# Two interleaved attention and FFT-filter layers on one core: which queue carries which rows, and where a few loads and transpositions stand in the order

## The chip, the core and the metric

The kernel runs on one core of one Trainium2 chip. The core has TensorE (PE in the profile) for matrix products and transpositions, VectorE (DVE), ScalarE (ACT) and GpSimd (POOL) for work on elements, and SyncE (SP), which only issues transfers. The metric is the device time of one launch in microseconds; the kernel before was timed in three runs.

## The reference

The input `x` has S = 2048 rows of D = 576 values, all in fp32. Four layers follow one another, attention and spectral filter in turn, each with a residual:

```
def _A_ref(x, wqkv, wo):                     # attention, 32 heads of 18, window W = 256
    q, k, v = (x @ wqkv) split into 3 x 32 heads
    scores = einsum("bhqd,bhkd->bhqk", q, k) * Dh ** -0.5
    scores = where(0 <= i - j < W, scores, -1e9)
    return einsum("bhqk,bhkd->bhqd", softmax(scores), v) merged @ wo

def _B_ref(x, w_r, w_i):                     # two-dimensional real FFT, a filter, and back
    X = rfft2(x, axes=(-2, -1)) * (w_r + 1j * w_i)
    return irfft2(X, s=(S, D), axes=(-2, -1))

x = x + _A_ref(layernorm(x), wqkv, wo)
x = x + _B_ref(layernorm(x), w_r, w_i)
x = x + _A_ref(layernorm(x), wqkv, wo)
x = x + _B_ref(layernorm(x), w_r, w_i)
```

## The kernel before

The order of the instructions on each engine is written by hand: the kernel records them one after another, and each engine works through its own in that order. Matrix products in fp32 accuracy are made from products of rounded values: an operand is split into a high part and a low part (`xh`, `xl`; `wqh`, `wql`), and two or three products are added.

**Transfers.** SyncE, ScalarE and GpSimd each issue transfers from their own place in the order. The transfers of SyncE and ScalarE together share eight completion semaphores, which are handed out in turn in the order of the program; a transfer is issued only when the one eight places earlier on that list, which has the same semaphore, has landed. GpSimd's transfers have eight of their own. What stands behind a waiting transfer on its engine waits too.

**Attention (`layer_a`).** The 2048 rows are 16 tiles of 128. In layer 1 `first_tiles` and the loop after it read each tile (`ld`), take its statistics (`bn`, `sq`, `bn2`), centre and scale it (`f0`, which gives `axn`), transpose it on TensorE (`f1`, tiles `tpaa` and `tpba`; ScalarE's and VectorE's casts give `xh` and `xl`) and make the value rows (`f2`, PSUM tile `vps`, stored to `v_d`). Then the projections of queries and keys run (`proj`, PSUM tile `pj`, copied through `sg` to memory `qk_d`). At their start ScalarE loads its table for the exponential by a one-column activation into the tile `ex`, and GpSimd builds the mask, clears parts of the key and query stacks by a long row of fills, and makes `wql`. In `opening` the first scores (`S`), their row maxima (`m`) and the remaining projections alternate; `m_rows` transposes four tiles of maxima (`tpm`), and ScalarE issues four transfers that put them into the query stack (`qs<-mt`). The exponentials are `E` (scores less the maximum, on TensorE) and `P` (ScalarE), the product with the values is `U`. At the end the attention's output blocks (`o_d` in memory) are loaded again by `out.load_o(u)`, GpSimd splits their last 64 columns, TensorE transposes them (`tpo`), and `out.unit` multiplies by `wo` (`ops`, 28 products); `out.load_x` loads the residual rows.

**Spectral filter (`layer_b`).** The transform along the 576 values is a product with cosine and sine tables; along the 2048 rows it is split as 16 x 128. *Forward columns*: for each tile n2 of 16, `f3` makes `pz` and `f4` the tile `ye` [128, 2 x 290]. It is stored to `yd[0][:, n2]` in memory. *Filter groups*: group g of 16 reads a tile of 128 rows, 8 from each n2 (`g0`), multiplies by `fc` (`g1m`, PSUM tile `p`), by the filter weights (VectorE, GpSimd: `uv`) and by `m` (`g2`, PSUM tile `pq`); the result (`ze` for odd, `eo` for even groups) goes to `yd[1][:, g]`. *Inverse*: tile n2 reads 128 rows, 8 of each group, into one of four places `yis` (`ly`), multiplies by `ga` (`i1`, PSUM tile `pi`), is transposed (`i2`, `tp`) and transformed back along the 576 values (`i3`, `po`).

At both changes of order between columns and groups the last results don't go through memory for all of their readers. From tile FD = 11 on, the eight rows of a tile that belong to groups 0 and 1 are sent straight into those groups' place in the on-chip memory ("rows", 8 x 580 values, 18.1 KB); rows of the tiles before come by one load. Likewise from group FG = 11 on the rows for the first `near` inverse tiles (two in layer 1, three in layer 2) are sent straight, and the older groups' rows come by two loads each, one of groups 0 to 7 and one of groups 8 to 10. All later groups and tiles load 128 rows from memory once every part of them is stored. While TensorE has nothing to do there in layer 2, it runs `warm` products whose result is not used; in layer 1 it prepares weights (`w1`, `w2`, PSUM tile `wo`) instead. In the profile the shared on-chip region in which the groups' places, `yis` and several other tiles lie is called `ofree` whatever tile it is.

## Time and profile before

| | us |
|---|---|
| three runs | 1385.17, 1386.48 (median), 1386.85 |
| the profiled execution | 1387.57 |
| its span in the profile | 1385.1 |
| TensorE busy in it | 1343.1 |
| VectorE busy | 893.3 |
| ScalarE busy | 785.4 |
| GpSimd busy | 640.0 |

TensorE's granted clock was 0.994 of full speed on average. In the rows below, a line of the order of time has its start, its duration, the engine, the line of the kernel, the operation, the tile written and the tiles read, and in brackets how long the engine had stood idle before it and what ended that. SPq, ACTq and POOL with DMA_DIRECT2D are the issue of transfers, and "xN" says that N like ones were merged. A row of waits has the waiting product, who was waited for, the total, the number of waits and the longest. A row of a stretch (A:B) has its length, the busy time of PE, PEld (weight loads), DVE, ACT and POOL with the number of instructions, the granted clock, the share of the DMA engines that was busy, and GB/s.

### The profile page before, as it was taken

How to read it: one execution, taken by the hardware profiler on the slowest of the kernel's cores; microseconds unless marked ns; L12 is line 12 of the kernel's file. 1: busy time of each engine (PE TensorE's matmuls, PEld its weight loads, DVE VectorE, ACT ScalarE, POOL GpSimd, SP SyncE). 2: the span in 40 equal slices, each digit the busy share in tenths (PEclk: the TensorE clock that was granted, in tenths of full speed). 3: DMA queues.
4: the chain of work that ended last, by engine and by line, in shares of the span. 5: the costliest groups of instructions: out<-in, count | busy, mean ns of one | idle time of the engine just before them, and what ended most of it. 6: DMA issues, size and time to landing. Idle time of an engine off the chain costs nothing.

```text
span 1385.1 us, 33553 instructions
## 1 busy us (share of the span) xinstructions
PE 1343.1 (97%) x11356; PEld 1001.1 (72%) x11356; DVE 893.3 (64%) x3046; ACT 785.4 (57%) x1978; POOL 640.0 (46%) x1140
## 2 busy tenths in 40 slices
PE   8999999999999999998999999999999999998988
PEld 8986666666665699975999866666666655897577
DVE  4417777877778266666673157787777883564745
ACT  5522777777778544443355316777777777563223
POOL 2257555555447443475221394554545457102711
PEclk9999999999999999999999999999999999999999
DMA  6756655655446457678763468555555465597864
GB/s 192 211 160 204 190 181 174 189 167 163 145 150 185 109 166 239 218 244 258 254 224 73 107 199 232 169 163 168 165 157 143 151 181 147 171 349 247 257 224 158
DMA packets 202159, 259.09 MB, mean 187 GB/s; under 512 B 104270, under 2 KB 109646, under 8 KB 201478
## 3 DMA queue, kind: packets, MB, share of 16 engines
q1 hardware_dynamic: 191494, 235.63, 55.8%
...
## 4 chain that ended last, share of the span: by engine, by line
PE 83%; DMA 5%; ACT 3%; DVE 3%; POOL 2%; issue 2%; SPq 1%; ACTq 0%; DVEq 0%; POOLq 0%
PE pj L1067 16%; PE S L1124 12%; PE U L1181 11%; PE vps L963 8%; PE ops L758 7%; PE E L1161 5%; PE po L251 4%; PE pq L488 2%; PE pf L251 2%; PE p L467 2%; PE tpo L1195 2%; PE pi L551 2%; ACT P L1162 2%; PE pz L289 2%; DMA yd<-ze 1%
## 5 line engine op out<-in xcount | busy, mean ns | idle before, releaser
L1126 DVE CUSTOM_DVE_ANT_0 jk<-S,mask 128x384 bf16<-128x384 f32 (+2 forms) x1024 | 490.4, 529 | 109.4 <-PE E L1161 56.1
L1162 ACT ACTIVATE P<-E 128x384 f32<-128x384 f32 (+2 forms) x1024 | 409.0, 476 | 121.9 <-PE E L1161 98.7
L1164 POOL TENSOR_SCALAR_AFFINE_SELECT P<-P 128x512 f32<-128x512 f32 x256 | 163.1, 637 | 277.9 <-ACT P L1162 254.3
L1124 PE MATMUL S<-ks,qs 63*128 63x384 f32 (+2 forms) x1024 | 269.1, 371 | 1.0 <-DVE m L1126 0.4
L1161 PE MATMUL E<-qs,ks 64*128 64x384 f32 (+2 forms) x1024 | 222.2, 372 | 3.3 <-ACT P L1162 2.6
L1124 PEld LDWEIGHTS S<-ks,qs 63*128 63x128 f32 x1024 | 140.7, 185 | 105.2 <-DVE m L1126 73.1
L1181 PE MATMUL U<-P,vq 128*19 128x128 f32 (+1 forms) x3840 | 187.8, 328 | 1.0 <-ACT us L1186 1.0
L1067 PE MATMUL pj<-xh,wqh 128*128 128x512 f32 x360 | 156.4, 434 | 3.3 <-DVE sg L1082 2.8
L1181 PEld LDWEIGHTS U<-P,vq 128*19 128x19 f32 x3840 | 95.7, 98 | 77.5 <-issue 21.7
L1167 POOL TENSOR_SCALAR_AFFINE_SELECT P<-P 128x512 f32<-128x512 f32 x224 | 142.8, 638 | 0.0
L1161 PEld LDWEIGHTS E<-qs,ks 64*128 64x128 f32 x1024 | 114.1, 185 | 17.0 <-ACT P L1162 8.2
L1067 PE MATMUL pj<-xh,wql 128*128 128x512 f32 x360 | 124.5, 419 | 0.5 <-POOL wql L648 0.5
L1067 PE MATMUL pj<-xl,wqh 128*128 128x512 f32 x288 | 122.1, 424 | 0.0
L758 PE MATMUL ops<-oroom 128*128 128x290 f32 (+1 forms) x812 | 116.3, 300 | 0.2
L758 PEld LDWEIGHTS ops<-oroom 128*128 128x128 f32 x812 | 111.4, 191 | 0.7 <-DVE ofree L781 0.7
L1067 PEld LDWEIGHTS pj<-xh,wqh 128*128 128x128 f32 x360 | 67.9, 189 | 34.8 <-issue 10.8
L1082 DVE TENSOR_TENSOR sg<-pj,sg 128x512 fp32r<-128x512 f32 x72 | 49.5, 687 | 58.3 <-ACT sg L1079 58.3
L1126 DVE DVE_READ_ACCUMULATOR2_ANT m<- 128x1 f32 x1024 | 85.2, 83 | 0.0
L1067 PEld LDWEIGHTS pj<-xh,wql 128*128 128x128 f32 x360 | 64.2, 189 | 20.9 <-issue 10.6
L1079 ACT CAST sg<-pj 128x512 fp32r<-128x512 f32 x72 | 42.2, 586 | 61.8 <-PE pj L1067 44.9
L243 ACT CAST et<-tp 128x512 fp32r<-128x512 f32 x53 | 31.2, 588 | 77.8 <-PE tp L239 76.7
L963 PE MATMUL vps<-wvh,xh 128*128 128x288 f32 x320 | 70.6, 302 | 0.2
...
## 6 DMA issues: line engine op xcount, KB each, us to landing
...
qs<-qk_d SPq DMA_DIRECT2D x384, 72.0 KB
...
```

Of the source, the lines that this page charges most:

```text
L251: T.matmul(ps[:, c, 0:NF], tail[r] if si == 4 else hl_(si), dcs[b // 2][r, b % 2], start=mi == si == 0, stop=si == 4)
L758: self.nc.tensor.matmul(self.ps[u][n][:, 0:self.n], x, self.w[p][:, (2 * wk + n) * self.n:(2 * wk + n + 1) * self.n], start=first and i == ...
L963: T.matmul(ps[:, n, 0:288], xT(xk, c), w[:, wk, n * 288:(n + 1) * 288], start=i == 0, stop=i == len(ks) - 1)
L1067: T.matmul(box["ps"].rearrange("r (n p) -> r n p", n=NT) if second else box["ps"], w[:, wk], x, start=s == 0, stop=s == len(ks) - 1)
L1082: V.tensor_sub(rest[:, 1], by, rest[:, 0].bitcast(F32))
L1124: T.matmul(ps[:, 0:N], q[b:b + 63, pair, i * 128:i * 128 + 128], k[b:b + 63, pair, lo:hi], start=True, stop=True)
L1126: V.tensor_tensor_reduce(out=jk[:, 0:N], in0=ps[:, 0:N], in1=mask[:, 384 - N:384], scale=1.0, scalar=-3e38, op0=ALU.add, op1=ALU.max, accu ...
L1161: T.matmul(ps[:, 0:nq], k[b:b + 64, pair, j * 128:j * 128 + 128], q[b:b + 64, pair, j * 128:j * 128 + nq], start=True, stop=True)
L1162: A.activation(p[:, hl_, 0:nq], ps[:, 0:nq], AF.Exp, scale=SC)
L1164: P.affine_select(out=p[:, :, 0:128], in_=p[:, :, 0:128], pattern=[[0, 4], [1, 128]], compare_op=ALU.is_ge, fill=0.0, base=0, channel_mult ...
L1167: P.affine_select(out=p[:, :, 256:384], in_=p[:, :, 256:384], pattern=[[0, 4], [-1, 128]], compare_op=ALU.is_gt, fill=0.0, base=0, channel ...
L1181: T.matmul(U[32 * h:32 * h + 19, (q0 % 4) * 128:(q0 % 4) * 128 + 128 * (q1 - q0)], vts[n][:, j, h], pt[n, j][:, h, (q0 - j) * 128:(q1 - j) ...
```

## The change

Six things change; the arithmetic stays.

1. *Groups to inverse tiles.* In layer 1 three tiles instead of two get their rows straight (`near` is 3 in both layers). GpSimd issues all rows for tile 2: of groups 11 to 13 in step 14, of groups 14 and 15 in step 15. In layer 2 that work was ScalarE's and, for group 15, SyncE's. The loads of groups 8 to 10 move from step 12 to step 13, behind the rows of group 12.
2. *Columns to groups in layer 2.* The rows of tiles 11 to 15 go to four groups, 0 to 3. So there are four rows a tile instead of two, a second load for the older tiles' rows, and no load for groups 2 and 3. Tile 13's rows and store are on GpSimd, tile 14's on ScalarE (recorded in the step of tile 15), tiles 11, 12 and 15's on SyncE; tile 15's store stands between its rows.
3. *`load_o(5)`* moves to the turn of the third block, ahead of the spectral layer, in both layers.
4. *`first_tiles`* in layer 1 holds `sq`, `bn2` and `f0` of tile 3, which came from the loop behind it.
5. *`ex`* is taken from the pool `bp` instead of `wp`.
6. *`m_rows`* in `opening` stands after three projection steps of the turn instead of after all seven.

In the order of SyncE in layer 2, from the columns to the groups, before: `ye` is the tile's result, `ofree<-ye` a row transfer, `yd0<-ye` the store, `ofree<-yd0` a load.

```order
L319 DMA ofree_17769<-ye11_19706 8x580 x2
L321 DMA yd0_18867<-ye11_19706 16x8x580
L327 DMA ofree_17769<-yd0_18867 88x2x580
L783 DMA x2_61<-ofree_17769 128x580
L319 DMA ofree_17769<-ye12_19777 8x580 x2
L319 DMA ofree_17769<-ye13_19791 8x580 x2
L319 DMA ofree_17769<-ye15_19813 8x580 x2
L321 DMA yd0_18867<-ye15_19813 16x8x580
L455 DMA ofree_17769<-yd0_18867 128x580 x2
L455 DMA ofree_17769<-yd0_18867 128x2x580 x5
```

And after:

```order
L321 DMA ofree_17775<-ye11_19712 8x580 x4
L326 DMA yd0_18874<-ye11_19712 16x8x580
L335 DMA ofree_17775<-yd0_18874 88x2x580 x2
L792 DMA x2_61<-ofree_17775 128x580
L321 DMA ofree_17775<-ye12_19786 8x580 x4
L326 DMA yd0_18874<-ye12_19786 16x8x580
L321 DMA ofree_17775<-ye15_19825 8x580 x2
L326 DMA yd0_18874<-ye15_19825 16x8x580
L321 DMA ofree_17775<-ye15_19825 8x580 x2
L464 DMA ofree_17775<-yd0_18874 128x580 x2
L464 DMA ofree_17775<-yd0_18874 128x2x580 x4
```

Tile 12 has four rows and its store on this queue, tile 13 none, tile 15 two more rows behind its store, and the two loads of 128 x 580 that were for groups 2 and 3 now serve groups 4 and 5.

On GpSimd at the same place, before (`ye<-half` is the subtraction that completes a tile):

```order
L653 TENSOR_TENSOR ofree_17769<-ofree_17769 128x64
L303 TENSOR_TENSOR ye12_19777<-half12_19765 128x290
L303 TENSOR_TENSOR ye13_19791<-half13_19792 128x290
L303 TENSOR_TENSOR ye14_19798<-half14_19799 128x290
L319 DMA ofree_17769<-ye14_19798 8x580 x2
L321 DMA yd0_18867<-ye14_19798 16x8x580
```

And after:

```order
L662 TENSOR_TENSOR ofree_17775<-ofree_17775 128x64
L303 TENSOR_TENSOR ye12_19786<-half12_19774 128x290
L303 TENSOR_TENSOR ye13_19803<-half13_19804 128x290
L321 DMA ofree_17775<-ye13_19803 8x580 x4
L326 DMA yd0_18874<-ye13_19803 16x8x580
L303 TENSOR_TENSOR ye14_19813<-half14_19814 128x290
L487 TENSOR_TENSOR uv0_19890<-ofree_17775 128x290
```

The five transfers of tile 13 now stand ahead of tile 14's subtraction, and tile 14's own have left this engine.

On SyncE in layer 1, from the groups to the inverse tiles, before: `ze` and `eo` are the groups' results (`eo2` is group 12's, `eo3` group 14's), `yd1` the memory between them, 24x580 the older groups' rows, 128x580 an inverse tile's load.

```order
L519 DMA ofree_7004<-yd1_8101 24x580 x2
L495 DMA ofree_7004<-eo2_8121 8x580 x2
L495 DMA ofree_7004<-ze13_10127 8x580 x2
L495 DMA ofree_7004<-eo3_8122 8x580
L495 DMA ofree_7004<-ze15_10153 8x580 x2
L525 DMA yd1_8101<-ze13_10127 16x8x580
L525 DMA yd1_8101<-ze15_10153 16x8x580
L164 DMA ofree_7004<-x0_59 128x1160
L545 DMA ofree_7004<-yd1_8101 128x580
L555 DMA x1_60<-ofree_7004 128x580
```

And after:

```order
L504 DMA ofree_7004<-eo2_8122 8x580 x2
L525 DMA ofree_7004<-yd1_8102 24x580 x3
L504 DMA ofree_7004<-ze13_10126 8x580 x2
L504 DMA ofree_7004<-eo3_8123 8x580
L504 DMA ofree_7004<-ze15_10158 8x580 x2
L534 DMA yd1_8102<-ze13_10126 16x8x580
L534 DMA yd1_8102<-ze15_10158 16x8x580
L164 DMA ofree_7004<-x0_59 128x1160
L564 DMA x1_60<-ofree_7004 128x580
L164 DMA ofree_7004<-x0_59 128x1160
L554 DMA ofree_7004<-yd1_8102 128x580
```

The rows of group 12 stand ahead of the older groups' loads, of which there are three instead of two, and the first load of 128 x 580 is tile 3's instead of tile 2's; it now stands behind tile 0's store to `x1`.

On SyncE in layer 2, at the end of the attention, before: `ofree<-o_d` of 128x448 is `load_o`.

```order
L724 DMA ofree_17769<-o7_d_10198 64x2048
L713 DMA ofree_17769<-o_d_10197 128x448
L724 DMA ofree_17769<-o7_d_10198 32x2048
L783 DMA x2_61<-ofree_17769 128x580 x3
L180 DMA ga_18890<-in_ga 128x256
L713 DMA ofree_17769<-o_d_10197 128x448 x3
L717 DMA ofree_17769<-x1_60 128x580
L783 DMA x2_61<-ofree_17769 128x580
```

And after:

```order
L722 DMA ofree_17775<-o_d_10204 128x448
L733 DMA ofree_17775<-o7_d_10205 32x2048
L722 DMA ofree_17775<-o_d_10204 128x448
L792 DMA x2_61<-ofree_17775 128x580 x3
L180 DMA ga_18897<-in_ga 128x256
L722 DMA ofree_17775<-o_d_10204 128x448 x2
L726 DMA ofree_17775<-x1_60 128x580
L792 DMA x2_61<-ofree_17775 128x580
```

One of the three loads behind `ga` stands ahead of the three stores to `x2` now.

The diff:

```diff
--- before.py
+++ after.py
@@ -138,7 +138,7 @@
     yd = [dram.tile([16, 16, 8, 2 * NF], F32, name=f"yd{j}") for j in range(2)]
     OPEN = *range(2, 17, 2), 17
     FD, FG, SH = 11, 11, 192
-    near, NY = (2, 3) if first else (3, 4)
+    near, NY = 3, 3 if first else 4
     with ExitStack() as stack:
         banks, inner = ExitStack(), ExitStack()
         ip = stack.enter_context(tc.tile_pool(name="bi", bufs=1))
@@ -148,7 +148,7 @@
         xfv, dstv = [a.rearrange("(p n) d -> p n d", n=NT) for a in (xf, dst)]
         xs, ys = {}, {}
 
-        pairs = [rl[:, 1160 * k:1160 * k + 1160] for k in range(4)]
+        pairs = [rl[:, 1160 * k:1160 * k + 1160] for k in (0, 3, 1, 2)]
         yis, tws = [[rl[:, at + 580 * k:at + 580 * k + 580].rearrange("p (a f) -> p a f", f=NF) for k in range(n)] for at, n in ((4640, 4), (6960, 2))]
 
         def y_tile(k):
@@ -305,26 +305,34 @@
                 both = ip.tile([128, 2, NF], F32, tag="both", name=f"half{n2}", bufs=2)
                 A.copy(both[:, 0], pz[:, 1, 0:NF])
                 if not first and n2 == NT - 1:
-                    for k in (n2 - 3, n2 - 2):
-                        hs[k]["store"](nc.scalar)
+                    hs[n2 - 1]["send"]()
                 V.tensor_add(ye[:, 0], pz[:, 0, 0:NF], both[:, 0])
                 V.tensor_sub(ye[:, 1], pz[:, 0, 0:NF], both[:, 0])
             yef = ye.rearrange("p j f -> p (j f)")
             pre(n2)
+            wide = 1 if first else 2
             if n2 == FD:
-                y_tile(0)
-            eng = P if n2 == NT - 2 else nc.sync
-            if n2 >= FD:
-                for g in range(2):
+                for k in range(wide):
+                    y_tile(k)
+            eng = nc.sync if n2 < NT - 3 or n2 == NT - 1 else P if first is (n2 == NT - 2) else nc.sync if first else nc.scalar
+
+            def rows(lo, hi):
+                for g in range(lo, hi):
                     eng.dma_start(ys[g][8 * n2:8 * n2 + 8].rearrange("p c f -> p (c f)"), yef[8 * g:8 * g + 8])
-            def store(q):
-                q.dma_start(yd[0][:, n2], yef)
-            if first or n2 not in (NT - 4, NT - 3):
-                store(eng)
+
+            def send():
+                if n2 >= FD:
+                    rows(0, 2 if n2 == NT - 1 else 2 * wide)
+                eng.dma_start(yd[0][:, n2], yef)
+                if n2 == NT - 1:
+                    rows(2, 2 * wide)
+            if eng is nc.scalar:
+                h["send"] = send
             else:
-                h["store"] = store
+                send()
             if n2 == FD:
-                nc.sync.dma_start(pairs[0].rearrange("p (a f) -> p a f", a=2)[0:8 * FD], yd[0][0:2, 0:FD].rearrange("a n i f -> (n i) a f"))
+                for k in range(wide):
+                    nc.sync.dma_start(pairs[k].rearrange("p (a f) -> p a f", a=2)[0:8 * FD], yd[0][2 * k:2 * k + 2, 0:FD].rearrange("a n i f -> (n i) a f"))
 
         def warm(n):
 
@@ -362,7 +370,7 @@
             f0(0, hs[0])
             for j in (1, 2, 3):
                 rims(j)
-            out.load(5)
+            out.load_x(5)
             norm(1)
             out.load(6)
             out.tail(5)
@@ -419,7 +427,8 @@
             zeros()
             norm(0)
             for u in (5, 6, 7):
-                out.load_o(u)
+                if u > 5:
+                    out.load_o(u)
                 out.tail(u)
             for u in (1, 2):
                 out.sums(u)
@@ -451,7 +460,7 @@
         def g0(g, h):
             if g % 2 == 0 and g not in ys:
                 y = y_tile(g // 2).rearrange("p a c f -> p a (c f)")
-                for a in ((0, 1), (1, 2)) if g == 2 else ((0, 2),):
+                for a in ((0, 1), (1, 2)) if g == (2 if first else 4) else ((0, 2),):
                     nc.sync.dma_start(y[:, a[0]:a[1]], yd[0][g + a[0]:g + a[1]].rearrange("a n i f -> (n i) a f"))
             h["y"] = ys[g]
 
@@ -500,23 +509,23 @@
                 V.tensor_sub(ye[:, 1], pq[:, 0, 0:NF], both[:, 1])
                 if first:
                     w1(3)
-                else:
-                    rows(nc.scalar, 2, 13)
-                    rows(nc.scalar, 2, 14)
-                for n2 in range(near):
+                for n2 in range(2):
                     rows(nc.sync, n2, 15)
+                for k in (14, 15):
+                    rows(P, 2, k)
                 held.pop()()
             else:
                 A.copy(both, pq[:, :, 0:NF])
-                if near > 2 and g in (FG + 1, FG + 2):
-                    rows(nc.scalar, 2, g - 1)
                 P.tensor_sub(ye[:, 1, 0:SH], both[:, 0, 0:SH], both[:, 1, 0:SH])
                 V.tensor_add(ye[:, 0], pq[:, 0, 0:NF], both[:, 1])
                 V.tensor_sub(ye[:, 1, SH:NF], pq[:, 0, SH:NF], both[:, 1, SH:NF])
-            if g in (FG - 1, FG + 1):
+            if g in (FG - 1, FG + 2):
                 lo, hi = (0, 8) if g < FG else (8, FG)
                 for n2 in range(near):
                     nc.sync.dma_start(yis[n2][8 * lo:8 * hi].rearrange("p c f -> p (c f)"), yd[1][n2, lo:hi].rearrange("g i f -> (g i) f"))
+            if g == 14:
+                for k in range(FG, 14):
+                    rows(P, 2, k)
             if FG <= g < 15:
                 for n2 in range(2):
                     rows(P if g == 14 and n2 else nc.sync, n2, g)
@@ -1006,6 +1015,9 @@
                 w_low(4)
                 bn(3, h[3])
                 f2(0, h[0], slice(1, 14))
+                sq(3, h[3])
+                bn2(3, h[3])
+                f0(3, h[3])
                 f2(1, h[1], slice(0, 8))
 
             if second:
@@ -1020,7 +1032,7 @@
                     if not second:
                         first_tiles()
                 for lag, fn in ((0, ld), (6 + late, f1), (4, sq), (4 + second, bn2), (4 + 2 * second, f0), (3, bn), (7 + late, f2)):
-                    if 0 <= s - lag < NT:
+                    if 0 <= s - lag < NT and (second or (s, lag) != (7, 4)):
                         fn(s - lag, hold[s - lag], *([slice(8, 14)] if s == 7 and lag == 6 and not second else []))
                 if s < 6 + late:
                     yield
@@ -1042,7 +1054,7 @@
                 q = wp.tile([128, 2, S], F32R, name=f"qs{j}", bufs=1)
                 k = wp.tile([128, 2, S], F32R, name=f"ks{j}", bufs=1)
                 qs.append(q); ks_.append(k)
-            A.activation(wp.tile([128, 1], F32, name="ex", bufs=1), eps, AF.Exp)
+            A.activation(bp.tile([128, 1], F32, tag="ex", name="ex", bufs=1), eps, AF.Exp)
 
             ended = []
 
@@ -1245,11 +1257,12 @@
                             score_max(t + LEAD, pair, hp)
                     remainders()
                     want = 7 * (t + LEAD + 1)
-                    yield from pj[n:want]
-                    n = want
                     y = t + LEAD - 1
+                    yield from pj[n:n + 3]
                     if y > 0 and y % 4 == 3:
                         m_rows(0, y // 4)
+                    yield from pj[n + 3:want]
+                    n = want
 
             def lasting(p):
                 x, half = p
@@ -1363,8 +1376,7 @@
                 if t - OB - 5 in (0, 1, 2):
                     u = t - OB - 5
                     out.turn(u, pp.tile([128, 512], F32, tag="pj", name=f"tpa{u}", bufs=1), V)
-                    if u < 2:
-                        out.load_o(u + 3)
+                    out.load_o(u + 3)
                 if t == NX:
 
                     A.activation(wp.tile([128, 1], F32, name="se", bufs=1), eps, AF.Sqrt)
```

## The prediction

> **What bounds the kernel now.** I read the share of busy time first, then TensorE's waits over the whole run, then the order of time around each place that the diff touches. The profiled execution took 1387.57 us (span 1385.1 us and 2.47 us around it), 1.09 us above the median 1386.48 us of the three runs, which spread from 1385.17 to 1386.85; so a difference under about 0.2% (2.8 us) can't be told from none.
>
> ```profile
> PE 1343.1 (97%) x11356; PEld 1001.1 (72%) x11356; DVE 893.3 (64%) x3046; ACT 785.4 (57%) x1978; POOL 640.0 (46%) x1140
> ...
> PE pi L551 <- DMA ofree<-yd: 4.3, 2, 3.0
> ...
> PE pj L1067 <- POOL wql L648: 0.5, 1, 0.5
> ```
>
> TensorE is busy 1343.1 of 1385.1 us. No part of the change removes arithmetic from it, so everything to be won lies in the 42 us in which it stands, and in stretches where its clock has dropped after such a stop. A wait row gives the total, the count and the longest; the two shown are the largest and a small one that decides a term below. The change touches many such stops, each at another place, so the sum has many small terms, and each place's rows stand with it.
>
> **First tiles of layer 1.** The centring of tile 3 now stands ahead of the casts of tile 2.
>
> ```profile
> 14.67 0.21 DVE L918 BATCH_NORM_AGGREGATE mv<-st 128x2 f32<-128x12 f32 x1
> 17.71 0.69 DVE L662 TENSOR_TENSOR xl<-tpaa,xh 128x512 fp32r<-128x512 f32 x1 [2.84 <-ACT xh L661]
> ...
> 19.62 0.66 PE L659 MATMUL tpaa<-ident,axn 128*128 128x128 f32 x4 [0.87 <-ACT axn L929]
> ```
>
> The tile's statistics are ready at 14.88 (14.67 + 0.21), but VectorE stands 2.84 us for the other tile's cast before it takes the next step of tile 3. With the order turned, the normalised tile is there some 2 us sooner and the stop of 0.87 goes. The cast, some 0.3 us late then, lies beside TensorE's value matmuls. Term: -0.9 (between -0.5 and -0.9).
>
> **The exp-table load.** Its small output tile `ex` no longer takes the memory of tiles that the stores to `v_d` read, so ScalarE needn't wait for them.
>
> ```profile
> 84.28 1.28 ACT L1045 ACT_TABLE_LOAD   x1 [4.20 <-DMA v_d<-vt]
> ...
> 87.09 0.50 PE L1067 MATMUL pj<-xh,wqh 128*128 128x512 f32 x1 [1.42 <-DVE sg L1082]
> ...
> 84.56 0.42 POOL L1035 MEMSET mask<- 128x384 bf16 x1 [13.61 <-DMA v_d<-vt]
> ...
> 108.35 1.54 POOL L648 TENSOR_TENSOR wql<-wqr,wqh 128x640 fp32r<-128x640 f32 x1
> ...
> 790.39 0.51 PE L1067 MATMUL pj<-xh,wqh 128*128 128x512 f32 x1 [0.60 <-DVE sg L1082]
> ```
>
> In layer 1 the stop of 1.42 goes, but it is not won: GpSimd's chain from the mask at 84.56 to `wql` at 108.35 also starts at those stores' landing, isn't touched, and TensorE already waits 0.5 for its end (the last wait row above). TensorE comes there 1.42 earlier and waits 1.9. In layer 2 the stop is 0.60, and no wait on `wql` is listed there (its count is 1), with no row for how near it is; I take half. Term: -0.3 (0 to -0.6).
>
> **The row of maxima.** The transposition `tpm` and what follows from it are recorded four projection matmuls sooner.
>
> ```profile
> 129.12 3.01 ACTq L1144 DMA_DIRECT2D qs<-mt  x4
> ...
> 129.55 1.07 PE L1067 MATMUL pj<-xh,wql 128*128 128x512 f32 x4
> 133.20 0.44 PE L1161 MATMUL E<-qs,ks 64*128 64x384 f32 x1 [1.59 <-ACT P L1162]
> ...
> 837.03 0.44 PE L1161 MATMUL E<-qs,ks 64*128 64x384 f32 x1 [1.01 <-ACT P L1162]
> ```
>
> ScalarE spends 3.01 us issuing the four transfers of the maxima; the cast and the exponentials stand behind them, and TensorE waits 1.59 and, in layer 2, 1.01. The same issue begins 4 matmuls earlier, about 0.23 us each by the start-to-start in the group of four that takes 1.07, so 0.9. It is a shift of ScalarE's queue with nothing before it that would be late. Term: -0.9 twice, -1.8 (-1.2 to -1.9).
>
> **The load of the sixth output block (`load_o(5)`) in layer 2.** It moves from the bunch of three at 1191.70 to the turn of the block before it.
>
> ```profile
> 1191.70 1.40 SPq L713 DMA_DIRECT2D ofree<-o_d  x3
> ...
> 1189.66 4.05 PE L758 MATMUL ops<-oroom 128*128 128x290 f32 x28
> 1195.05 0.52 PE L733 MATMUL tpo<-ident,ofree 128*128 128x128 f32 x3 [1.34 <-DMA ofree<-o_d]
> 1196.13 0.33 PE L734 MATMUL tpo<-ident,ofree 128*128 128x128 f32 x1 [0.56 <-POOL ofree L653]
> ...
> 1197.70 4.97 PE L758 MATMUL ops<-oroom 128*128 128x290 f32 x28
> ...
> 1195.00:1200.00 5.00, 4.39 (x21) 4.19 (x22) 3.55 (x9) 4.07 (x14) 2.00 (x6) 0.66 0.23 78
> 1200.00:1255.00 55.00, 55.00 (x419) 55.00 (x418) 36.50 (x97) 33.32 (x94) 4.50 (x16) 1.00 0.98 341
> ```
>
> Two stops, 1.34 for the load and 0.56 for GpSimd's split of it, are gone when it is there early. Behind them the granted clock was 0.66 (a stretch's row ends with the granted clock, the share of the DMA engines and GB/s), and the 28 matmuls took 4.97 where the 28 before took 4.05: another 0.92. By these rows the edit is worth up to 2.8; I take 2.7, as the clock may drop a little without them too. The lower end is 1.9, the stops alone. Late next are the loads of blocks 6 and 7, issued about as now and wanted one and two rounds of 28 matmuls later. Term: -2.7 (-1.9 to -2.8). In layer 1 the same move meets no stop in the rows, so 0.
>
> The Trainium skill ("TensorE: Matmul & The Clock Gate", Part 1: The HAM clock gate) says that the clock falls to half only after a window of about 3.4 us without work. Here stops of 1.34 and 0.56 us with work between were enough for 0.66, so the trace doesn't agree; by the page the drop would have another cause and stay, and this term would be -1.9 and the sum 0.8 smaller.
>
> **Layer 1, filter groups to inverse tiles.** Tile 2 now gets its rows like tiles 0 and 1 and needs no load of 128 rows; GpSimd issues them. The older groups' loads stand behind the rows of group 12.
>
> ```profile
> 643.74 1.35 SPq L495 DMA_DIRECT2D ofree<-eo  x2
> ...
> 647.32 1.30 SPq L495 DMA_DIRECT2D ofree<-ze  x2
> ...
> 653.26 0.34 SPq L545 DMA_DIRECT2D ofree<-yd  x1
> ...
> 649.47 2.20 PE L551 MATMUL pi<-ofree,ga 128*128 128x290 f32 x8 [1.75 <-DMA ofree<-ze]
> ...
> 657.22 2.22 PE L551 MATMUL pi<-ofree,ga 128*128 128x290 f32 x4 [3.02 <-DMA ofree<-yd]
> ...
> 662.48 1.14 PE L551 MATMUL pi<-ofree,ga 128*128 128x290 f32 x4
> ```
>
> Row group 12 (1.35) now goes out while SyncE still waits to issue the older loads, of which there is one more (some 0.3): the last rows, now at 647.32, come about 1.0 sooner, and with them tiles 0 and 1 (stop 1.75). Tile 2 no longer waits for the load issued at 653.26, so its stop of 3.02 goes, and its four matmuls, slow after that stop (2.22 against 1.14 for tile 3's), gain 1.1. Together 5.1. The first load that still is one is tile 3's. It takes the place of tile 2's, a little earlier, and lands about 4 us after issue as that one did (653.26 to 657.22), near 656. It now stands behind tile 0's store in the queue, which waits for that tile's sum, near 651 by the row of 649.47 less 1.0, and so isn't later for it; tile 3 is then due at 662.48 - 5.1 = 657.4. That is tight, so I take -4.5. If GpSimd's seven transfers land as late as the removed load did, only the first 1.0 is left. Term: -4.5 (-1.0 to -5.2). From tile 3 on TensorE is the bound, so what is won there stays.
>
> **Layer 2, the same place.** It had three such tiles already; new are GpSimd as issuer, one row less at the end of SyncE's queue and the loads' place.
>
> ```profile
> 1313.42 1.59 SPq L495 DMA_DIRECT2D ofree<-eo  x2
> ...
> 1317.25 1.98 SPq L495 DMA_DIRECT2D ofree<-ze  x3
> ...
> 1323.95 0.80 SPq L545 DMA_DIRECT2D ofree<-yd  x2
> ...
> 1329.79 1.25 PE L551 MATMUL pi<-ofree,ga 128*128 128x290 f32 x4 [1.25 <-DMA ofree<-yd]
> ```
>
> The pair at 1313.42 (1.59) goes into an idle time ahead, and the third of the rows at 1317.25 (1.98 / 3 = 0.66) leaves the queue: 2.25 less ahead of the last store, on whose landing the load at 1323.95 waits, and that load ended TensorE's wait at 1329.79. The tiles ahead of it start sooner by the same rows, about 1.4. Term: -2.1 (-0.5 to -2.3).
>
> **Layer 2, columns to filter groups.** The rows of tiles 11 to 15 go to four groups, not two; so the load for groups 2 and 3, after the last store, is not needed. The price is ten more row transfers, on three queues.
>
> ```profile
> 1261.14 6.67 SPq L319 DMA_DIRECT2D ofree<-ye  x6
> 1269.26 0.58 SPq L321 DMA_DIRECT2D yd<-ye  x1
> 1272.44 9.29 SPq L455 DMA_DIRECT2D ofree<-yd  x6
> ...
> 1263.06 1.52 ACTq L321 DMA_DIRECT2D yd<-ye  x2
> ...
> 1263.88 1.12 POOL L319 DMA_DIRECT2D ofree<-ye  x2 [0.29 <-DMA ofree<-yd]
> ...
> 1269.66 0.71 PE L467 MATMUL p<-ofree,fc 128*64 128x290 f32 x4 [2.16 <-DMA ofree<-ye]
> ...
> 1271.64 1.19 PE L467 MATMUL p<-ofree,fc 128*64 128x290 f32 x8
> 1275.36 2.20 PE L467 MATMUL p<-ofree,fc 128*64 128x290 f32 x8 [2.53 <-DMA ofree<-yd]
> ```
>
> Today groups 0 and 1 start at 1269.66 after a stop of 2.16, group 2 at 1275.36 after 2.53. After the change tile 13's four rows and store stand on GpSimd ahead of tile 14's subtraction: 5 x 0.56 = 2.8, so tile 14's transfers, now on ScalarE, begin near 1263.88 + 2.8 = 1266.7, last row at 1269.0, store at 1269.7 (0.76 each). SyncE issues tile 12's and 15's rows, and the eight completion semaphores go round over SyncE's and ScalarE's transfers in the order of the program: a transfer waits until the one eight places before has landed. So tile 12's second row waits for tile 14's first, and tile 15's for the last of them. With landings of 2 to 3 us (the last of the six rows ends its issue at 1267.81 and the data is used at 1269.66; the store issued at 1269.26 lets the load go at 1272.44) tile 15's first two rows go at about 1271.7 and 1272.4, and group 0 starts near 1274.2: 4.5 later. The stop of 2.53 then is gone, but TensorE has stood 6.7 us (since 1269.66 - 2.16 = 1267.5) and starts slow, as group 2 does now (2.20 for eight matmuls, 1.19 for the eight before). The matmuls of groups 0 and 1, 3.2 us now (1269.66 to 1272.83), take about 4.8, slow for most of it, so group 2 comes at 1279.0, 3.6 later than now, and no longer slow: 2.20 - 1.19 = 1.0 back. Term: +2.5. Bounds: -4.7, both stops gone; +5.0, all of the delay and the slow start.
>
> **Sum.** -0.9 - 0.3 - 1.8 - 2.7 - 4.5 - 2.1 + 2.5 = -9.8, so 1387.57 - 9.8 = 1377.8 for a profiled execution, and 1376.7 beside the median.
>
> **Rivals.** (a) The last hand-over works as it was drawn: the rows land in time, both stops go. For it, each row transfer is small; against it, the chain over the shared semaphores. 2.5 + 4.7 = 7.2 less: 1369.5. (b) GpSimd's rows for the third inverse tile land late, and both places at the inverse yield 1.5 together in place of 6.6: 1381.8. For it, the last of them are issued behind six others; against it, they start about 9 us before tile 2 is due. (c) From 1200 to 1255 the DMA engines were 0.98 busy: when TensorE arrives 2.7 earlier they are the bound and the gain of `load_o(5)` is given back: 1379.4. Against it, TensorE had no gap in those 55 us. (d) Slower: the waits on the shared semaphores in the hand-over from columns to groups stand in a row instead of beside each other, six issues of SyncE (three rows and the store of tile 12, two rows of tile 15) at a landing of 3.2 (1269.26 to 1272.44), 19 us, of which the rows of now already fill 2: +17 in place of +2.5, 1391.2. It decides from a loss of 12.3 on, where the other terms are used up, and needs group 0 to start after about 1284.
>
> **How the numbers follow.** The forecast 50%, (a) 15%, (b) 16%, (c) 10%, (d) 9%. The range reaches from (a) to somewhat above (b), where (b) and (c) fall together with the upper bound of the hand-over: 1369.5 to 1385.0; only (d) is left out. Faster 86%: all but (d), less the upper edge of (b); same 5%, slower 9%.
>
> **What would show it.** Right: no wait for `axn` of 0.87 near 19.6, none of 1.4 near 87 but about 1.9 for `wql` near 108; the exp wait of 1.59 down to 0.7; `tpo` near 1195 without a stop and the clock there near 1.0; `pi` of tile 2 in layer 1 without a wait and of tile 3 about 5 us sooner beside the work before it; group 0 of layer 2 later and group 2 without a stop. Wrong: tile 2's `pi` waits for a row from GpSimd, or the stop ahead of group 0 is far longer than 6.7 us, or short.

## The result, and the profile after

| | runs | median, us | ratio to before, 95% |
|---|---|---|---|
| before, on the same chip | 14 | 1385.38 | |
| changed | 14 | 1384.74 | 0.9996 (0.9984 to 1.0008) |
| changed, beside the first experiments | 12 | 1382.50 (before 1382.37) | 0.9995 (0.9979 to 1.0011) |

Nothing that can be told from no change, where 9.8 us were forecast. The profiled execution of the changed kernel took 1384.23 us (span 1382.3). The page's busy times and the waits of TensorE on the changed kernel:

```profile
PE 1341.2 (97%) x11356; PEld 998.3 (72%) x11356; DVE 892.7 (65%) x3046; ACT 786.9 (57%) x1978; POOL 646.4 (47%) x1152
...
PE p L476 <- DMA ofree<-ye: 8.7, 1, 8.7
PE pj L1079 <- POOL wql L657: 2.4, 2, 1.9
...
PE tpo L742 <- ACT ofree L799: 1.1, 1, 1.1
PE E L1173 <- DMA qs<-mt: 1.1, 2, 0.9
...
PE pi L560 <- DMA ofree<-yd: 1.1, 1, 1.1
```

The stops that were to go did go: no 3.0 for the inverse load of layer 1, none of 1.4 at the first projection copies, none of 1.3 for the sixth output block. Others stand in their place, with other names: 8.7 ahead of the filter groups of layer 2 (2.2 and 2.5 before), 1.9 for `wql` (0.5 before), 1.1 for ScalarE one output block later, 0.9 for a transfer of the maxima, 1.1 for the next inverse load.

One profile doesn't tell how much each of these counts. So all later runs were compared stretch by stretch. A stretch's length is the start of one product less the start of an earlier one, the same two products in every profile; stretches are named by these starts in the first profile of before. The fifth column is the mean of the profiles that have the part less the mean of those that have it not, with the number of profiles of each in brackets.

| stretch, us | before, three profiles | changed, two | that part undone | mean with less mean without (profiles) | forecast |
|---|---|---|---|---|---|
| 14 to 112, first tiles and exp table | 98.8, 98.9, 98.8 | 99.3, 99.6 | 98.8 | -0.4 (11, 5) | -0.9 |
| 125 to 141, maxima, layer 1 | 16.0, 15.8, 14.7 | 14.1, 14.1 | 14.3 | -0.9 (13, 5) | -0.9 |
| 640 to 664, groups to inverse, layer 1 | 23.5, 22.4, 23.7 | 21.3, 20.5 | 22.8 | -1.9 (12, 4) | -4.5 |
| 815 to 888, maxima, layer 2 | 73.0, 75.2, 73.6 | 74.7, 75.3 | 73.7 | +1.2 (13, 5) | -0.9 |
| 1190 to 1204, sixth output block | 14.5, 12.3, 12.2 | 12.0, 12.0 | 12.2 | -0.8 (14, 4) | -2.7 |
| 1255 to 1280, columns to groups, layer 2 | 25.2, 23.8, 23.2 | 29.2, 28.4 | 24.3 | +4.6 (9, 4) | +2.5 |
| 1304 to 1331, groups to inverse, layer 2 | 27.0, 28.5, 26.1 | 24.2, 24.0 | 26.3 | -3.2 (14, 4) | -2.1 |

The means are over all profiles, of the experiments too, that have that part or have it not; profiles in which an experiment alters the same place in another way are left out. They add up to -1.4, within the interval of the measured time (-0.6, from -2.2 to +1.1). Outside these stretches the profiles differ too: from 141 to 640 by up to 3.6 us between one execution and another of kernels that are alike there, from 888 to 1140 by up to 3.3. Kernels below for which no ratio is given ran once, for their profile; a single time says little where 14 runs of one kernel spread over 6 us.

### The profile page after: what moved, and what is told of

Its sections match the earlier page's. It is cut to its first block, busy times and chain, and to the rows that moved or that the text cites. A ratio compares the mean times of both kernels' runs of the same rounds, so it can differ in the third digit from the quotient of the medians.

```text
span 1382.3 us, 33597 instructions
## 1 busy us (share of the span) xinstructions
PE 1341.2 (97%) x11356; PEld 998.3 (72%) x11356; DVE 892.7 (65%) x3046; ACT 786.9 (57%) x1978; POOL 646.4 (47%) x1152
## 4 chain that ended last, share of the span: by engine, by line
PE 81%; POOL 4%; DMA 4%; ACT 4%; DVE 3%; issue 3%; SPq 1%; ACTq 0%; DVEq 0%; POOLq 0%
PE pj L1079 15%; PE S L1136 12%; PE U L1193 11%; PE vps L972 8%; PE ops L767 7%; PE E L1173 5%; PE po L251 4%; PE p L476 2%; PE pf L251 2%; PE tpo L1207 2%; PE pi L560 2%; PE pq L497 2%; ACT P L1174 2%; POOL qs L1227 2%; POOL ks L1226 2%
## 5 line engine op out<-in xcount | busy, mean ns | idle before, releaser
L1079 PEld LDWEIGHTS pj<-xh,wql 128*128 128x128 f32 x360 | 64.8, 190 | 23.5 <-issue 10.7
```

The costliest lines, as they stand in the source:

```text
L1079: T.matmul(box["ps"].rearrange("r (n p) -> r n p", n=NT) if second else box["ps"], w[:, wk], x, start=s == 0, stop=s == len(ks) - 1)
```

## Experiments

**Once more the changed kernel, and twice more the one before.**

> The changed kernel once more, beside the experiments, to see which small differences between the two profiles come back. If the profile of the changed kernel can be relied on to a few tenths at a place, the stop ahead of group 0 in layer 2 is again 8.7 us (8.2 to 9.2), the one for wql in layer 1 1.9, the one for the maxima's transfer near 883 0.9, and the inverse of layer 1 gives back 1.1 at tile 3. If these are of one execution only, they differ by half or more. Time against before: 0.998 to 1.001.

> The kernel before once more, for a second profile of it. Two profiles of the changed kernel differed by 1.7 us in span, and in single waits for transfers of the attention by up to 1.6. If the first profile of before was an ordinary one, this one's span is within 1 us of 1385.1 and its stops are the same at each place; if it was a slow one, the span is 1380 to 1383 and the difference lies in the waits for transfers, not at the places of the change.

> The kernel before a third time. Its first two profiles differ by 1 to 3 us in single stretches (648 to 664: 1.1; 842 to 888: 1.6; 1190 to 1204: 2.2; 1255 to 1280: 1.5; 1304 to 1331: 1.5). If the second was the ordinary one, the third has no drop of the clock near 1195 and takes about 12.0 from 1190 to 1204; if the first was, it has the drop again and takes 14.

Spans 1384.0, 1385.4 and 1382.4 us. At the first repeat the stops of 8.7, 1.9 and 0.9 came back as 8.1, 1.9 and 1.3, the 1.1 at inverse tile 3 only as 0.4. The second expectation was half wrong: the span was as long as the first, but the length lay elsewhere, two of the changed places among them. The third's span was 3 us shorter, and it too had no drop of the clock near 1195. What the table shows for before is therefore no fixed number at any place where a transfer's landing decides.

**The columns' rows for two groups again.**

```diff
-                    hs[n2 - 1]["send"]()
+                    for k in (n2 - 3, n2 - 2):
+                        hs[k]["store"](nc.scalar)
...
-                for k in range(wide):
-                    y_tile(k)
+                y_tile(0)
...
-            if eng is nc.scalar:
-                h["send"] = send
+            if first or n2 not in (NT - 4, NT - 3):
+                store(eng)
```

> The changed kernel with the rows of layer 2's columns for two groups again, as before the change; all else stays. Theory 1: this part costs 4.3 us (group 3's products stood at -4.2 ahead of it and +0.1 behind it in the profiles), so without it the kernel takes 1380 to 1381, ratio 0.996 to 0.998, with a stop of about 2.2 ahead of group 0 and 2.5 ahead of group 2. Rival: what this place gains or loses is made up later, at the inverse tiles whose loads wait for the last store; then the time stays within 1 us of the changed kernel's.

1379.71 us, ratio 0.9975 (0.9957 to 0.9993): without this part the rest of the change is a gain of some 3 us. That is 2.8 under the changed kernel's 1382.50, where theory 1 had 4.3, and the intervals of the two ratios overlap; the time alone wouldn't settle it. The stretch does: from 1255 to 1280 it is 24.3 instead of 29.2 and 28.4, with stops of 2.06 and 3.17 in place of the one of 8.66. Theory 1 holds at this place.

**Where the 4.6 come from.** The changed kernel at that place, SyncE, ScalarE, GpSimd and TensorE in order of time, then a stretch's row, then the chain of work that ended last there (start, duration, what):

```profile
1259.27 9.63 SPq L321 DMA_DIRECT2D ofree<-ye  x4
1269.62 1.30 SPq L321 DMA_DIRECT2D ofree<-ye  x2
...
1262.88 2.78 ACTq L321 DMA_DIRECT2D ofree<-ye  x4
...
1259.49 2.09 POOL L321 DMA_DIRECT2D ofree<-ye  x4 [0.41 <-DVE ye L302]
...
1272.43 1.24 PE L476 MATMUL p<-ofree,fc 128*64 128x290 f32 x4 [8.66 <-DMA ofree<-ye]
...
1268.00:1276.00 8.00, 3.57 (x16) 2.15 (x18) 0.00 (x0) 0.00 (x0) 0.00 (x0) 0.57 0.48 122
...
1262.88 4.01 DMA ofree<-ye
...
1266.92 0.63 SPq L321
...
1269.62 2.47 DMA ofree<-ye
```

SyncE spends 9.63 us on the four rows of tile 12: it stands until the first row of tile 14, issued by ScalarE at 1262.88, has landed 4.01 us later, on the semaphore they share. Tile 15's rows follow at 1269.62, land after 2.47, and TensorE, which stood 8.66 us, goes on at a clock of 0.57. Four other orders of the same transfers tell whether the semaphores or the transfers are at fault.

GpSimd's transfers of tile 13 behind the subtraction of tile 14:

```diff
                 P.tensor_sub(ye[:, 1], both[:, 0], both[:, 1])
+                if n2 == NT - 2:
+                    hs[n2 - 1]["send"]()
...
-            if eng is nc.scalar:
+            if not first and n2 in (NT - 3, NT - 2):
                 h["send"] = send
```

> The changed kernel with one thing put in another order: tile 13's five transfers on GpSimd stand behind the subtraction of tile 14, not ahead of it. Theory 1 (the delay of 2.8 us of tile 14's rows passes through the shared semaphores to tile 12's and 15's rows): tile 14's rows on ScalarE begin 2.9 us sooner, SyncE's rows follow, group 0 starts 2.5 to 3.5 sooner, the stop falls from 8.7 to about 5.5, time 1381 to 1382.5. Rival (the many small transfers themselves land late, whatever their order): the stop stays over 7.5 and the time within 1 us of the changed kernel's.

1383.22 us, ratio 1.0011 (0.9995 to 1.0027). ScalarE's order of time, the chain, and TensorE's:

```profile
1257.65 2.83 ACTq L323 DMA_DIRECT2D ofree<-ye  x4
...
1260.52 7.01 DMA yd<-ye
...
1267.59 2.04 DMA ofree<-ye
...
1269.87 1.24 PE L478 MATMUL p<-ofree,fc 128*64 128x290 f32 x4 [8.35 <-DMA ofree<-ye]
```

ScalarE's rows do start sooner (warm products end at about 1261.5 here, 1263.8 in the changed kernel), and nothing is won: now it is ScalarE's store of tile 14 that takes 7.01 us to land, and tile 15's rows go out on SyncE when it has. As a forecast this missed, and the rival's two numbers came true (a stop over 7.5, a time within 1 us). The rows show the mechanism of theory 1 with another transfer to wait for; the next two runs tell the two apart.

Tiles 13 and 14 both on GpSimd, nothing on ScalarE:

```diff
-            eng = nc.sync if n2 < NT - 3 or n2 == NT - 1 else P if first is (n2 == NT - 2) else nc.sync if first else nc.scalar
+            eng = P if n2 == NT - 2 or not first and n2 == NT - 3 else nc.sync
...
-                if not first and n2 == NT - 1:
-                    hs[n2 - 1]["send"]()
```

> The changed kernel with tiles 13 and 14 both on GpSimd, all ten transfers behind tile 14's subtraction, and none of them on ScalarE. With tile 13's transfers moved alone the stop ahead of group 0 had stayed (8.35): SyncE's rows of tile 15 then waited 7.0 us for tile 14's store on ScalarE. Theory 1 (SyncE's rows are held by landings of another engine's transfers through the shared semaphores): with no transfer of ScalarE among them SyncE issues the rows of tile 15 by about 1263 (1269.6 in the changed kernel), and group 0 then waits only for GpSimd's rows: stop 4 to 6.5. Rival (the rows land late since the transfers as a whole take that time): the stop stays over 7.5.

```profile
1258.88 2.69 SPq L321 DMA_DIRECT2D ofree<-ye  x4
...
1262.51 2.77 SPq L321 DMA_DIRECT2D ofree<-ye  x2
...
1268.85 0.84 PE L476 MATMUL p<-ofree,fc 128*64 128x290 f32 x4 [3.89 <-DMA ofree<-ye]
```

The four rows of tile 12 take 2.69 us instead of 9.63, and the stop is 3.89. The same number of rows is moved. So the larger part of the stop came through the shared semaphores, and the rival, which had a stop over 7.5, falls. Slow landing is what is left: seven of GpSimd's eight rows took 4.5 to 5.7 us to land here.

The rows of all four tiles ahead of all their stores, tiles 13's and 14's stores on ScalarE:

```diff
+                h["rows"] = lambda: rows(0, 4)
+                if n2 != NT - 3:
+                    rows(0, 4)
+                if n2 == NT - 1:
+                    for k, q in ((12, nc.sync), (13, nc.scalar), (14, nc.scalar), (15, nc.sync)):
+                        hs[k]["store"](q)
```

> As the run with both tiles on GpSimd, and the four tiles' rows stand ahead of all their stores: tile 12's and 15's stores on SyncE behind its rows, 13's and 14's on ScalarE behind. Theory 1: nothing that SyncE's rows wait for is in flight but their own forerunners, and the stores of 290 KB are no longer ahead of them; group 0 starts 4 to 6 us sooner than in the changed kernel and groups 2 and 3 follow without a stop; time 4 to 5 us under the changed kernel's, ratio to before 0.996 to 0.998. Rival (small transfers are slow in themselves, 4 to 6 us each): stop over 6, gain under 2.

```profile
1260.67 6.21 DMA yd<-ye
...
1266.96 2.32 DMA ofree<-ye
...
1272.07 1.24 PE L484 MATMUL p<-ofree,fc 128*64 128x290 f32 x4 [6.95 <-issue]
```

1384.50 us, ratio 1.0006 (0.9987 to 1.0025): a miss again, once more with the rival's numbers, and the clearest row of all for the semaphores. "Ahead" held only on each queue: ScalarE, which had nothing else to do, sent a store at 1260.67, and SyncE's first row of tile 12, whose data had long been ready, stood until that store had landed 6.21 us later.

GpSimd issues the eight rows of tiles 13 and 14, SyncE all the rest, stores last (the lines are against the run before):

```diff
-                    for k, q in ((12, nc.sync), (13, nc.scalar), (14, nc.scalar), (15, nc.sync)):
+                    for k, q in ((12, nc.sync), (13, nc.sync), (14, nc.sync), (15, nc.sync)):
...
+                    for lo in (0, 2):
+                        for k in (n2 - 1, n2):
+                            hs[k]["rows"](lo, lo + 2)
```

> The changed kernel with another hand-over from columns to groups in layer 2. GpSimd issues the eight rows of tiles 13 and 14 (groups 0 and 1 first), SyncE the rows of 12 and 15, then SyncE the stores of 12 to 15; ScalarE issues nothing there. In the run with the rows ahead of the stores, ScalarE's stores of 13 and 14 went out first and SyncE's first row waited 6.2 us for one of them on the shared semaphore, so the stop was 6.95. Theory 1 (shared semaphores): nothing of another engine is left to wait for; the stop ahead of group 0 falls to 2 to 4, and the stretch from 1255 to 1280 takes 4 to 6 us less than in the changed kernel (there +4.0 and +3.2 against before). Time 1378 to 1381, ratio 0.996 to 0.999. Rival (small transfers slow, or GpSimd's queue): stop over 5.

```profile
1262.17 5.56 DMA ofree<-ye
...
1267.86 0.72 PE L486 MATMUL p<-ofree,fc 128*64 128x290 f32 x4 [2.47 <-DMA ofree<-ye]
```

1378.20 us, ratio 0.9955 (0.9941 to 0.9970); stop 2.47, the stretch 23.1. As expected. With four groups served and no transfer of another engine in the ring, the hand-over is 5.7 us shorter than the mean with the changed order. It is 1.0 shorter than the mean of the four profiles with two groups, but only 0.1 shorter than the shortest of them. The first line is a row of tile 15 in the chain: issued by SyncE, it took 5.56 us to land, and that ends the stop now.

**First tiles and exp table.** Both undone, and both kept with a shorter row of fills:

```diff
-                sq(3, h[3])
-                bn2(3, h[3])
-                f0(3, h[3])
...
-            A.activation(bp.tile([128, 1], F32, tag="ex", name="ex", bufs=1), eps, AF.Exp)
+            A.activation(wp.tile([128, 1], F32, name="ex", bufs=1), eps, AF.Exp)
```

> The changed kernel with the first tiles' order and the exp table's tile as they were before. Theory: both gains are lost at GpSimd's row of fills, so nothing changes at 112 in layer 1 (within 0.5 of the changed kernel), in layer 2 at most 0.5 is lost; time within 1.0 of the changed kernel's. Rival: they are worth what their stops were, 0.9 + 1.4 + 0.6, and the time is 2 to 3 us longer.

```diff
-                    P.memset(ks_[i][b:b + 32, :, 512 * c:512 * c + 512].bitcast(F32), 1.0)
+                    (V if k < 2 else P).memset(ks_[i][b:b + 32, :, 512 * c:512 * c + 512].bitcast(F32), 1.0)
```

> The changed kernel with four of the fills that GpSimd does ahead of wql (ones for the key stack, first two projections) on VectorE, which is nearly idle there. Theory: the gain of the first tiles and of the exp table (2.7 us at 87) was lost at 108 because GpSimd's row of fills ends no earlier; with four fills of 0.95 less the wait of 1.9 for wql is gone, and at 112 the kernel stands 2.3 to 2.8 ahead of before in place of 0.0; layer 2 gains 0.5. Time 1381.5 to 1383. Rival: another wait takes its place there (VectorE's copies late, or the next split), and at 112 it stands under 1 ahead.

The changed kernel, with three stretches around its stop; then the run below that undoes the inverse hand-over (`no1`) and does the same as the changed kernel here; then the one with both parts undone; then the one with four fills on VectorE:

```profile
107.05 1.53 POOL L657 TENSOR_TENSOR wql<-wqr,wqh 128x640 fp32r<-128x640 f32 x1
108.64 2.07 PE L1079 MATMUL pj<-xh,wql 128*128 128x512 f32 x4 [1.87 <-POOL wql L657]
...
105.00:108.40 3.40, 1.76 (x9) 0.86 (x8) 2.35 (x17) 0.00 (x0) 3.28 (x4) 1.00 0.66 228
108.40:111.80 3.40, 3.17 (x8) 2.13 (x10) 0.00 (x0) 0.20 (x1) 3.30 (x5) 0.50 0.54 153
111.80:115.20 3.40, 3.40 (x18) 2.30 (x17) 3.10 (x12) 0.38 (x1) 3.33 (x5) 1.00 0.64 150
```

```profile
108.06 1.20 PE L1079 MATMUL pj<-xh,wql 128*128 128x512 f32 x4 [1.87 <-POOL wql L657]
...
108.00:111.40 3.40, 3.34 (x15) 2.39 (x16) 1.29 (x5) 0.59 (x1) 3.30 (x5) 1.00 0.64 168
```

```profile
109.53 1.21 PE L1076 MATMUL pj<-xh,wql 128*128 128x512 f32 x4 [0.46 <-POOL wql L657]
```

```profile
103.61 1.56 POOL L657 TENSOR_TENSOR wql<-wqr,wqh 128x640 fp32r<-128x640 f32 x1
...
106.85 1.09 PE L1079 MATMUL pj<-xh,wql 128*128 128x512 f32 x4
```

TensorE comes to the product with `wql` earlier and waits the difference. But `wql` came sooner too (107.05; 108.35 before), by 1.1 in the mean over the profiles, counted from the product at 14; so that much is passed on. Whether it is kept depends on the clock. All eleven profiles with both parts have this stop (1.81 to 1.87). In seven of them, the changed kernel's two among them, the clock is 0.50 for 3.4 us from about there on, the products run slowly (2.07 instead of 1.09 to 1.21 for four), and the stretch is 98.9 in the mean, as without the parts. In four it stays at 1.00, as in `no1`, and the stretch is 97.7. In the five profiles without the parts, where the stop is 0.47, the clock never fell here. The mean over all eleven is 98.4, without 98.8. With four fills less ahead of it, `wql` is ready 3.4 sooner, the wait and the drop are gone and the stretch is 95.3: the gain is 3.1 and stays. The times: 1386.32 us with both undone (ratio 1.0018, 1.0001 to 1.0034), 1381.23 with the fills moved (0.9985, 0.9970 to 1.0001). The first is some 3 us above the changed kernel, which is the rival's size, where the profiles show 0.4, which is the theory's; the two intervals touch, and it stays open whether that is chance.

**The maxima.** The move undone, and undone together with the two parts above:

```diff
-                    yield from pj[n:n + 3]
+                    yield from pj[n:want]
+                    n = want
                     if y > 0 and y % 4 == 3:
                         m_rows(0, y // 4)
-                    yield from pj[n + 3:want]
-                    n = want
```

> The changed kernel with the row of maxima at its old place. In all profiles of the changed family the stretch from 125 to 141 took 1.9 less than before. Theory: that is the move of the maxima, and with the old place it is 0 again (within 0.3); in layer 2 the stretch from 830 to 888 is the same within 0.5 as with the move, since there TensorE afterwards waits for other transfers of the maxima and gives it back. Rival: layer 2's gain of about 0.5 is kept, and the stretch gets longer by it or more.

> The changed kernel without the first tiles' order, the exp table's tile and the move of the maxima. With either the first two or the last undone the stretch from 125 to 141 still took 1.9 or 1.7 less than before, and its clock was 1.00; in both profiles of before a stop of 1.5 to 1.6 near 133 was followed by a clock of 0.51 and 0.70. Theory: any of the moves shortens that stop enough to keep the clock; with all three undone the stop is 1.5 again, the clock drops and the stretch takes 1.7 to 2.1 longer than in the changed kernel. Rival: something else in the change does it, and the stretch stays as in the changed kernel.

The changed kernel, the one with the move undone, and the second and third of before:

```profile
132.16 0.44 PE L1173 MATMUL E<-qs,ks 64*128 64x384 f32 x1 [0.53 <-ACT P L1174]
...
134.88 0.44 PE L1173 MATMUL E<-qs,ks 64*128 64x384 f32 x1 [0.44 <-ACT P L1174]
...
883.08 0.89 PE L1173 MATMUL E<-qs,ks 64*128 64x384 f32 x3 [0.93 <-DMA qs<-mt]
```

```profile
132.85 0.44 PE L1173 MATMUL E<-qs,ks 64*128 64x384 f32 x1 [1.04 <-ACT P L1174]
```

```profile
135.00:138.50 3.50, 3.50 (x16) 1.97 (x17) 1.90 (x7) 1.25 (x3) 1.22 (x2) 0.70 0.82 258
```

```profile
132.72 0.44 PE L1161 MATMUL E<-qs,ks 64*128 64x384 f32 x1 [1.51 <-ACT P L1162]
...
135.00:138.50 3.50, 3.50 (x19) 2.14 (x20) 2.89 (x11) 2.41 (x6) 1.66 (x3) 1.00 0.82 260
```

Both expectations failed on layer 1. With the move undone the stretch is 14.3 (1.7 under the first profile of before), and 14.3 too with all three undone. The move takes the stop from about 1.1 to 0.5 and adds one of 0.4 at the next exponential, 0.2 in sum. The rest is the clock: after stops of 1.59 and 1.52 it fell (0.51 and 0.70 in the stretch from 135.0 to 138.5; the drop of the second began at 133.7, so that row holds only part of it), after 1.51, 1.15 and 1.04 it didn't; that is chance in the profiles without the move, and the move's stop of 0.5 was never followed by it. In layer 2 the move is a loss, not the draw of the first theory: from 815 to 888 the kernel is 1.2 slower with it. 0.7 of that lies at the end of the stretch. There TensorE stands 0.6 to 1.8 for the maxima of the next block in nine of thirteen profiles with the move; without it, it stood there only in the second of before (0.8). 0.5 lies near 850: the same products take 6.4 to 7.5 us with the move and 6.4 in each profile without. That half of the loss, and the four profiles with the move that are as long without the wait for the maxima, stay unexplained.

**The sixth block's load at its old place.**

```diff
-                if u > 5:
-                    out.load_o(u)
+                out.load_o(u)
...
-                    out.load_o(u + 3)
+                    if u < 2:
+                        out.load_o(u + 3)
```

> The changed kernel with the sixth block's load at its old place. Theory: with the load early the stop of 1.1 moves from the load to ScalarE's normalisation one block later, so the early load is worth only what the drop of the clock and GpSimd's split cost in the first profile of before, which the second did not have; the stretch from 1190 to 1204 is 0.2 to 0.6 longer than in the changed kernel. Rival: the drop comes with the late load as a rule, and the stretch is 2 to 2.8 longer.

The changed kernel, then this run, then a stretch of the second profile of before:

```profile
1193.50 3.94 PE L767 MATMUL ops<-oroom 128*128 128x290 f32 x28
1198.57 0.52 PE L742 MATMUL tpo<-ident,ofree 128*128 128x128 f32 x3 [1.13 <-ACT ofree L799]
```

```profile
1194.27 0.52 PE L741 MATMUL tpo<-ident,ofree 128*128 128x128 f32 x3 [0.99 <-DMA ofree<-o_d]
1195.96 3.94 PE L766 MATMUL ops<-oroom 128*128 128x290 f32 x28
```

```profile
1195.00:1200.00 5.00, 3.76 (x29) 3.32 (x28) 2.37 (x7) 4.06 (x12) 2.16 (x6) 1.00 0.60 202
```

The theory holds: 12.2 against 12.0. The stop for the load is gone and one of 1.13 for ScalarE's normalisation stands one block later. With the late load the stop is 1.0 to 1.3, and the clock dropped in one profile of four.

**Groups to inverse tiles.** This part undone in both layers; and the load of tile 3 one step sooner:

```diff
-    near, NY = 3, 3 if first else 4
+    near, NY = (2, 3) if first else (3, 4)
...
-            if g in (FG - 1, FG + 2):
+            if g in (FG - 1, FG + 1):
...
-            if g == 14:
-                for k in range(FG, 14):
-                    rows(P, 2, k)
```

> The changed kernel with the hand-over from groups to inverse tiles as before in both layers. Theory: this part gains about 2 in layer 1 (648 to 664, between the two profiles of before and the mean of the changed family) and 3 to 4 in layer 2 (1304 to 1331); so here the first stretch is 1.5 to 3 longer than in the changed kernel, the second 2 to 4.5 longer. Rival: its gain is only that the first profile of before was slow at both; then both differ by under 1.

```diff
-            if n2 >= near:
+            if n2 >= near + first:
...
+            if first and n2 == 1:
+                nc.sync.dma_start(yis[3].rearrange("p c f -> p (c f)"), yd[1][3].rearrange("g i f -> (g i) f"))
```

> The changed kernel with only the load of inverse tile 3 in layer 1 one step sooner. In the changed kernel that load was issued at 652.76, behind tile 0's store and a load of 594 KB, landed after 6.8 us, and tile 3 waited 1.1 for it. Theory: the place behind those two is what costs it; the wait for tile 3 is under 0.3. Rival: the DMA engines are busy there anyway (0.80 of them), and the wait stays over 0.8.

The changed kernel in layer 1 and layer 2, then the undone one, then the sooner load:

```profile
652.76 0.34 SPq L554 DMA_DIRECT2D ofree<-yd  x1
...
649.30 2.19 PE L560 MATMUL pi<-ofree,ga 128*128 128x290 f32 x8 [1.90 <-issue]
...
653.87 1.15 PE L560 MATMUL pi<-ofree,ga 128*128 128x290 f32 x4
...
659.55 1.25 PE L560 MATMUL pi<-ofree,ga 128*128 128x290 f32 x4 [1.10 <-DMA ofree<-yd]
...
1327.11 1.25 PE L560 MATMUL pi<-ofree,ga 128*128 128x290 f32 x4
```

```profile
656.03 2.07 PE L560 MATMUL pi<-ofree,ga 128*128 128x290 f32 x4 [2.32 <-DMA ofree<-yd]
```

```profile
648.83 3.88 PE L562 MATMUL pi<-ofree,ga 128*128 128x290 f32 x8 [2.07 <-DMA ofree<-eo]
...
659.51 1.15 PE L562 MATMUL pi<-ofree,ga 128*128 128x290 f32 x4
```

The part is a gain: undone, the stretches are 22.8 and 26.3 against means of 21.2 and 23.8 with it. In layer 1, tile 2 starts without a stop, as meant. The last rows are issued 1.0 sooner but land no sooner (tiles 0 and 1 still wait 1.90): these tiles start 9.4 us behind the product at 640 in the mean, and 8.6 without the part. Tile 3's load, issued at 652.76, lands 6.8 us later and not 4. In layer 2 the clock fell to half for 3.4 us in each of the four profiles without the part and in none of the fourteen with it. The load one step sooner ends tile 3's wait, as that theory said; in that execution tiles 0 and 1 ran at half speed after their own stop (3.88 for eight), and the stretch, 21.9, is no shorter. So what the early load is worth alone stays open.

**The three remedies together.**

> That hand-over, four fills ahead of wql on VectorE, and in layer 1 the load of inverse tile 3 issued one step sooner (ahead of tile 0's store and of the second load of x). If the three give-backs are separate, it gains 4 to 6, 3.4 and 1.0 on the changed kernel: 1373 to 1377, ratio to before 0.993 to 0.996. Rival: less than 4 in all, since later waits for transfers take it back.

1374.95 us, ratio 0.9931 (0.9918 to 0.9943): 8 to 11 us under the kernel before, and, as the changed kernel takes the same time as that one, some 10 under the changed kernel too. Its lengths are 95.3 for 14 to 112, 23.2 for 1255 to 1280, 20.0 for 640 to 664. The give-backs were separate, and the forecast of 1373 to 1377 holds.

## Why the prediction was wrong

It forecast 1376.7 and 86% for faster; the time is the same. Its likeliest case failed, and so did the chances. That 1384.74 still lies inside the range, 0.3 under its upper end, is luck: that end stood for (b) and (c) together with the worst of the last hand-over, and neither (b) nor (c) came. (By the prediction's own terms the three together give 1387.0, so the range was also drawn too short.) By the stretches the sum is 8 us too good; the largest misses are the inverse of layer 1 (2.6), the maxima (2.1), the last hand-over (2.1) and the sixth block's load (1.9). The steps:

- *First tiles, -0.9.* The mechanism was right: the stop went, and some 1.1 was won, since GpSimd's chain came forward too. It was kept in four profiles of eleven and lost to the clock in seven, as the next point says.
- *The exp table, -0.3.* In layer 1 the wait for `wql` was foretold as 1.9 and is 1.87. The step that failed is the one that let TensorE's earlier arrival cost nothing: behind this stop the clock was at half for 3.4 us in seven of eleven profiles, behind the old one of 0.47 in none of five, and a drop lengthened the stretch by 1.3. The first tiles and the exp table together gave -0.4; they were not run apart. In layer 2 the stop of 0.60 went and 0.6 is waited for `wql` instead; from 787 to 815 the means differ by -0.2.
- *The row of maxima, -1.8.* The step that failed is "a shift of ScalarE's queue with nothing before it that would be late". What is late is behind it: a second exponential in layer 1, and in layer 2 the maxima of the next block, with as much again that is not explained. -0.9, most of it the clock, which had fallen in two of the five profiles without the move, and +1.2.
- *The sixth block's load, -2.7.* Failed, and by the whole term but for 0.2 in three of four profiles. Of the 2.7, 0.8 was a clock drop of one execution and 0.56 a wait of that execution alone. The 1.34 moved to ScalarE, which the prediction had not asked; it named the loads of blocks 6 and 7 as late next, and these came in time. The Trainium skill ("TensorE: Matmul & The Clock Gate", Part 1: The HAM clock gate) would have left the drop out of the sum, as its window of about 3.4 us without work was not reached; three of the four profiles with the late load agree, with a clock of 1.00, and the first doesn't. Nor do the seven profiles with a drop at the stop of 1.9 before `wql`.
- *Layer 1, groups to inverse, -4.5.* The mechanism was right, the size was not: -1.9. Two landings were taken too short. The last rows were to bring tiles 0 and 1 forward by 1.0; they were issued that much sooner, took longer to land, and the tiles start 0.8 later. Tile 3's load was to land in 4 us and took 6.8.
- *Layer 2, the same, -2.1.* Right in kind, and larger: -3.2. The stop of 1.25 that was read was a small one; in the second profile of before it was 3.58. And the term had nothing for the clock, which fell in every profile without the part and in none with it.
- *Columns to groups, +2.5.* The mechanism was right in every link (GpSimd, ScalarE, the shared semaphores, the clock), the size was not: +4.6. A landing of 2 to 3 us was taken; ScalarE's row took 4.0, and the stop was 8.7 and not 6.7.
- *Rivals.* (a) did not come. (b) did not come as drawn: tile 2 waits for no row of GpSimd, and the two places yield 5.1 in place of 6.6, not 1.5. (c) did not, TensorE being busy 55.00 of 55 us from 1200 to 1255 again. (d) named the right place and did not reach its price.

The sum failed as a sum. Six of its seven terms have one sign and were read from the stops of one execution, which took 1387.57 us where the median of 14 is 1385.38. Over the seven stretches of the table that profile is 1.1 us longer than the second of before and 5.7 longer than the third, and each of its stops was booked as a gain.
